# Attention: values in half pieces, k in rows of four keys, and another order for the first loads

## The chip, the cores and the metric

The kernel runs on one core of a Trainium2 chip. The metric is the device time of one execution in microseconds; of three runs the median counts. A core has five engines that work side by side, each with its own instruction queue: PE (matrix products), DVE (vector), ACT (activation functions), POOL and SP. SP does no arithmetic here; it issues DMAs. ACT issues some too. The DMAs of both queues run on the same 16 DMA engines. Engines wait for one another through semaphores.

## What is computed

Softmax attention for 16 x 32 = 512 heads in bfloat16, with 192 queries and 1024 keys of 128 elements in each head:

```python
B, H, Sq, Sk, D = 16, 32, 192, 1024, 128
scale = q.shape[-1] ** -0.5
scores = jnp.einsum("bhqd,bhkd->bhqk", q, k) * scale
p = _softmax(scores, axis=-1)
return jnp.einsum("bhqk,bhkd->bhqd", p, v)
```

The order of the keys doesn't matter, as long as a head's scores and its values are taken in the same order. k and v are 134 MB each, q and the output 25 MB each.

## The kernel before

**Tiles.** The heads are worked in 32 groups of 16 (`G`), a group in 8 pairs of heads, a pair in three units of 128 query rows: A (128 rows of one head), B (128 rows of the other) and S (64 rows of each). So there are 24 units a group. For a unit, PE multiplies q and k into 128x1024 scores in PSUM (`qk`, L270), DVE scales and copies them and finds each row's maximum in one instruction (L333), ACT takes the exponential (L374; for two units in six POOL subtracts the maximum first, L208, and ACT takes the exponential later), PE transposes the result in eight blocks of 128 keys (`tr`, L283), ACT brings the blocks back to SBUF (L383, L385), PE multiplies them by the values (`pv`, L317), and DVE divides by the row sums (L358). The order of the units on PE, DVE and ACT is written out by hand (`PE_ORDER` and its sisters, L17 to L20).

**Loads.** `kt` holds k transposed, `qt` q transposed, `vs` the values; each has two slots (`NS`), used by turns. k and q come by transposing DMAs on SP's queue (`load_kq`, L145), which put 128 elements of the head dimension on the partitions. A row of the k transpose is eight neighbouring keys (2048 bytes), so block t of a head's transposed keys has keys t, 8 + t, 16 + t and so on. The values come so that partition p has keys 8p to 8p + 7, one piece of 2048 bytes for each head and partition (`load_v`, L136). Both give the same order of keys.

**Order on SP.** After the start SP runs, for each group g: wait until the scores of group g are all done, issue k and q of group g + 2 into the slot that became free (`loads`, L157), then wait for group g's outputs and issue its stores in three DMAs by partitions (`stores`, L166, `STORE_PARTS`). The values of group g + 2 are issued by ACT, in its order of work, after unit 15 of group g + 1; it waits there until group g's products with values are done and until k of group g + 2 has landed (L391 to L394). A waiting instruction holds up everything behind it in its queue.

**The first two groups** have their own code. Group 0 comes in three parts by `FIRST`, heads 0 to 1, 2 to 7 and 8 to 15, in this order on SP's queue: k and q of the first part; k and q of the second; values of the first and of the second; k and q of the third; values of the third (L177 to L182). Group 1's k, q and values follow on the same queue. PE waits for each part's k and q before its first scores (L253) and for each part's values before its first product with them (L309).

Of the kernel before, what the change touches and what calls it, by code (L numbers as in the profile page):

```python
# [5 lines left out]
BF16 = mybir.dt.bfloat16  # L6
# [25 lines left out]


def _attention_kernel(nc, q, k, v, out, G=16, NS=2, NSS=5, NX=4, NPT=5,
                      FIRST=((0, 2), (2, 8), (8, 16)), LAST=((0, 4), (4, 6), (6, 7), (7, 8)), STORE_PARTS=((0, 80), (80, 124), (124, 128)), VALUES_AFTER=("ev", 15)):
    B, H, SQ, D = q.shape
    SK = k.shape[2]
    assert D == 128 and SK == 1024 and SQ == 192, (D, SK, SQ)
# [6 lines left out]
    KT_TILES = SK // 128  # L45
# [6 lines left out]
    kf = k.rearrange("b h s d -> (b h) s d")  # L52
    vf = v.rearrange("b h s d -> (b h) s d")
    of = out.rearrange("b h s d -> (b h) s d")

    def shifted(u):
        return UNITS[u % 6] in SHIFTED
# [12 lines left out]
    with ExitStack() as es:  # L70
        def sb(name, shape, dt):
            return es.enter_context(nc.sbuf_tensor(name, shape, dt))
# [4 lines left out]
        def sem(name):  # L77
            return es.enter_context(nc.semaphore(name))

        kt = sb("kt", [128, NS, KT_TILES, G * 128], BF16)  # L80
        qt = sb("qt", [128, NS, G * SQ], BF16)
        vs = sb("vs", [128, NS, G, KT_TILES, 128], BF16)
        ob = sb("ob", [128, NSO, PPG, 3, 128], BF16)
        ss = sb("ss", [128, NSS, SK], F32)
        nb = sb("nb", [128, NSS], F32)
# [11 lines left out]
        sxq = [sem("sxq%d" % i) for i in range(NS)]  # L97
        svl = [sem("svl%d" % i) for i in range(NS)]
        sf = [sem("sf%d" % i) for i in range(len(FIRST))]
        sfv = [sem("sfv%d" % i) for i in range(len(FIRST))]  # L100
        sst = [sem("sst%d" % i) for i in range(NSO)]
        s_qk = sem("s_qk")
        s_max = sem("s_max")
# [10 lines left out]
        def unit_info(u):  # L114
            name = UNITS[u % 6]
            pr = 2 * (u // 6) + int(name[1])
            return pr, "ABS".index(name[0]), pr // PPG, pr % PPG
# [6 lines left out]
        def load_cnt(g):  # L124
            return 16 * (g // NS + 1 - (g % NS == 0))
# [10 lines left out]
        def load_v(e, g, a, b, sm):  # L136
            h0 = g * G
            e.dma_start(  # L138
                vs[:, g % NS, a:b],
                vf[h0 + a:h0 + b].rearrange("g (p t) d -> p g t d", t=KT_TILES),  # L140
            ).then_inc(sm, 16)

        @block.sync
        def _(e):
            def load_kq(g, a, b, sems):  # L145
                s = g % NS
                h0 = g * G
                e.dma_start_transpose(  # L148
                    kt[:, s, :, a * 128:b * 128],
                    kf[h0 + a:h0 + b].rearrange("g (p t) d -> (g p) (t d)", t=KT_TILES),  # L150
                ).then_inc(sems[0], 16)
                e.dma_start_transpose(  # L152
                    qt[:, s, a * SQ:b * SQ],
                    qf[h0 + a:h0 + b].rearrange("g r d -> (g r) d"),
                ).then_inc(sems[1], 16)

            def loads(g):  # L157
                s = g % NS
                last_u = (g - NS + 1) * UPG - 1
                if g >= NS:  # L160
                    e.wait_ge(s_qk, last_u + 1)
                load_kq(g, 0, G, (sxk[s], sxq[s]))
                if g < NS:
                    load_v(e, g, 0, G, svl[s])

            def stores(g, a, b):  # L166
                so = g % NSO
                e.wait_ge(s_on, g * PPG + b)
                rows = of[g * G + 2 * a:g * G + 2 * b].rearrange("h r d -> (h r) d").rearrange(
                    "(n p) d -> p n d", p=128)  # L170
                for lo, hi in (((0, 128),) if g == NGR - 1 else STORE_PARTS):
                    e.dma_start(
                        rows[lo:hi],
                        ob[lo:hi, so, a:b].rearrange("p pg y d -> p (pg y) d"),
                    ).then_inc(sst[so], 16)

            n = len(FIRST)  # L177
            for i in range(n):
                load_kq(0, *FIRST[i], (sf[i], sf[i]))
                if i > 0:  # L180
                    for i2 in range(i if i > 1 else 0, i + 1):
                        load_v(e, 0, *FIRST[i2], sfv[i2])  # L182
            for g in range(1, min(NS, NGR)):
                loads(g)
            for g in range(NGR):
                if g + NS < NGR:
                    loads(g + NS)
                for a, b in (LAST if g == NGR - 1 else ((0, PPG),)):
                    stores(g, a, b)
            for so in range(min(NSO, NGR)):  # L190
                n = len(range(so, NGR - 1, NSO)) * len(STORE_PARTS)
                if so == (NGR - 1) % NSO:
                    n += len(LAST)
                e.wait_ge(sst[so], 16 * n)
# [23 lines left out]
        def _(pe):  # L218
# [19 lines left out]
            def qk(u):  # L238
                pr, k3, g, pg = unit_info(u)
                s = g % NS  # L240
                a = 2 * pg
                b = 2 * pg + 1
                S = s_ps[u % 2]
                if k3 < 2:
                    x0 = a * SQ if k3 == 0 else b * SQ + 64
                    tiles = [((0, 0), slice(0, 128), a if k3 == 0 else b, qt[:, s, x0:x0 + 128])]
                else:
                    tiles = [
                        ((0, 0), slice(0, 64), a, qt[:, s, a * SQ + 128:a * SQ + 192]),
                        ((0, 64), slice(64, 128), b, qt[:, s, b * SQ:b * SQ + 64]),  # L250
                    ]
                if g == 0:
                    for i, (h, _) in enumerate(FIRST):  # L253
                        if h <= b and i not in seen_kq:
                            seen_kq.add(i)
                            pe.wait_ge(sf[i], 32)
                elif u % UPG == 0:
                    pe.wait_ge(sxq[s], load_cnt(g))
                ins = None
                for c in range(2):  # L260
                    cs = slice(4 * c, 4 * c + 4)
                    for at, ps_, x, w in tiles:
                        if c == 0:
                            pe.ldweights(w, tile_position=at)  # L264
                            if at[1] == 0:
                                if g > 0 and u % UPG == 0:
                                    pe.wait_ge(sxk[s], load_cnt(g))
                                if u >= 2:
                                    pe.wait_ge(s_max, u - 1)
                        ins = product(S[ps_, cs], w, kt[:, s, cs, x * 128:x * 128 + 128], at)  # L270
                ins.then_inc(s_qk, 1)

            def tr(u):
# [12 lines left out]
            def pv(u):  # L286
                pr, k3, g, pg = unit_info(u)
                s = g % NS
                O = o_ps[pr % 2]
                PTS = pt_sb[:, u % NPT]  # L290
                sl = O_SLOT[k3]
                a = 2 * pg
                b = 2 * pg + 1
                ins = None
                with_rs = shifted(u)
                if k3 < 2:
                    tiles = [((0, 0), slice(0, 128), a if k3 == 0 else b)]
                else:
                    tiles = [((0, 0), slice(0, 64), a), ((0, 64), slice(64, 128), b)]
                pe.wait_ge(s_ev, u + 1)  # L300
                for t in range(KT_TILES):
                    first = t == 0
                    last = t == KT_TILES - 1
                    for at, rows, x in tiles:
                        w = PTS[:, t, rows]
                        pe.ldweights(w, tile_position=at)  # L306
                        if first and at[1] == 0:
                            if g == 0:
                                for i, (h, _) in enumerate(FIRST):  # L309
                                    if h <= b and i not in seen_v:  # L310
                                        seen_v.add(i)
                                        pe.wait_ge(sfv[i], 16)
                            elif u % UPG == 0:
                                pe.wait_ge(svl[s], load_cnt(g))
                            if k3 == 0 and pr >= 2:
                                pe.wait_ge(s_on, pr - 1)
                        ins = product(O[rows, sl, :], w, vs[:, s, x, t, :], at, first, last)  # L317
                        if with_rs:
                            ins = product(O[rows, 3, sl: sl + 1], w, ones[:, 0:1], at, False, last)
                ins.then_inc(s_pv, 1)  # L320
# [112 lines left out]
```

## Time and profile before

| | |
|---|---|
| three runs | 1200.33, 1194.54, 1207.98 us; median 1200.33 |
| the profiled execution | 1195.41 us, span 1193.6 |
| granted TensorE clock | 0.984 |
| busy: PE, DVE, ACT, POOL | 1127.5, 1088.2, 1082.4, 485.8 us |
| DMA | 321.26 MB, mean 269 GB/s |
| DMA from issue to landing, median | k 21.1, q 8.4, values on ACT's queue 16.3 us |

The span runs from the first to the last instruction of the profiled execution. "Busy" is the union of an engine's instructions. A line of a group or of the timeline has the source line (L148 is line 148), the engine (SPq is SP's queue), the operation and what it writes and reads (out<-in). In brackets stands the engine's idle time before it and what ended it. A row of the waits has the total, the number and the longest. DMA share is the mean busy share of the 16 DMA engines; it can pass 1, since pieces overlap. From the trace's record of single DMA pieces one can count how many of each size start in a stretch of time.

### The profile page before, as it was taken

The page shows a single profiled execution, that of the slowest core. Times are in us where ns is not written, and L with a number is a line of the kernel's source. Part 1 is how long each engine was busy: PE and PEld are TensorE (multiplying, and loading weights), DVE is VectorE, ACT ScalarE, POOL GpSimd, SP SyncE. Part 2 cuts the span into 40 slices and gives each one's busy share as a digit, 9 for nine tenths or more (in the row PEclk, how much of TensorE's full clock was granted, in tenths as well). Part 3 has the DMA queues.
Part 4 walks back from the last instruction along what each step waited for, and adds up shares of the span by engine and source line. Part 5 has one row for each costly group of instructions (what it writes and reads, how often), then busy time and mean ns, then how long its engine had stood idle before and what let it go on. Part 6 is the DMA issues. An engine that isn't in the chain of part 4 may idle for free.

```text
span 1193.6 us, 38884 instructions
## 1 busy us (share of the span) xinstructions
PE 1127.5 (94%) x18432; PEld 847.8 (71%) x15360; DVE 1088.2 (91%) x2304; ACT 1082.4 (91%) x1793; POOL 485.8 (41%) x262
## 2 busy tenths in 40 slices
PE   5698999999989999999999999999999999999998
PEld 2476767777767777777776777777777777777766
DVE  5587989999989999999998999999999999999987
ACT  4677989999999999999997999999999999999988
POOL 2233434434434434444443444444344344444432
PEclk9888999999999999999998999999999999999999
DMA  9999999999999999999999999999999999999991
GB/s 234 243 282 268 270 248 247 288 297 290 288 256 267 275 304 281 285 276 274 289 283 280 266 251 279 295 303 278 275 265 268 292 284 290 271 271 277 291 245 41
DMA packets 790348, 321.26 MB, mean 269 GB/s; under 512 B 724641, under 2 KB 724641, under 8 KB 790177
## 3 DMA queue, kind: packets, MB, share of 16 engines
q1 hardware_dynamic: 728257, 192.95, 83.9%
q10 hardware_dynamic: 61920, 125.83, 28.9%
q8 instruction: 132, 2.16, 0.7%
q14 instruction: 39, 0.32, 0.1%
HBM read 134.22 MB, written 25.17 MB: 134 GB/s over the span
## 4 chain that ended last, share of the span: by engine, by line
PE 58%; DMA 29%; ACT 7%; SPq 5%; issue 0%; DVE 0%
PE o_ps L221 21%; PE pt_ps L221 19%; DMA vs<-in_v_dram 19%; PE s_ps L221 18%; DMA qt<-in_q_dram 11%; SPq L148 5%; ACT x_sb L374 4%; ACT pt_sb L385 2%; ACT pt_sb L383 1%; SPq L152 0%; SPq L138 0%; DVE ob L358 0%; DVE rinv L356 0%
## 5 line engine op out<-in xcount | busy, mean ns | idle before, releaser
L333 DVE TENSOR_SCALAR_CACHE_REDUCE ss<-s_ps 128x1024 f32<-128x1024 f32 x768 | 920.4, 1220 | 89.1 <-PE s_ps L221 72.8
L208 POOL TENSOR_TENSOR x_sb<-ss,nb 128x1024 bf16<-128x1024 f32 x256 | 485.1, 1895 | 695.9 <-DVE ss L333 665.7
L374 ACT ACTIVATE x_sb<-ss,nb 128x1024 bf16<-128x1024 f32 x512 | 585.4, 1145 | 12.9 <-DVE ss L333 12.9
L306 PEld LDWEIGHTS <-pt_sb 128*128 128x128 bf16 (+1 forms) x8192 | 443.2, 104 | 213.5 <-issue 115.6
L221 PE MATMUL s_ps<-kt,qt 128*128 128x512 bf16 (+1 forms) x2048 | 467.9, 386 | 47.5 <-DMA qt<-in_q_dram 47.0
L221 PE MATMUL o_ps<-vs,pt_sb 128*128 128x128 bf16 (+1 forms) x8192 | 497.5, 219 | 14.2 <-DMA vs<-in_v_dram 13.9
L221 PE MATMUL pt_ps<-ident,x_sb 128*128 128x128 bf16 x6144 | 453.1, 220 | 1.3 <-ACT pt_sb L383 1.3
L280 PEld LDWEIGHTS <-x_sb 128*128 128x128 bf16 x6144 | 367.5, 98 | 62.5 <-issue 62.1
L385 ACT ACTIVATE pt_sb<-pt_ps 128x512 f32<-128x512 f32 x512 | 306.2, 598 | 78.7 <-PE pt_ps L221 77.8
L383 ACT ACTIVATE pt_sb<-pt_ps 128x1024 bf16<-128x1024 bf16 x256 | 260.4, 1017 | 14.4 <-PE pt_ps L221 14.3
L221 PE MATMUL o_ps<-ones,pt_sb 128*128 128x1 bf16 x2048 | 191.2, 166 | 0.0
L358 DVE TENSOR_TENSOR ob<-o_ps,rinv 128x384 bf16<-128x384 f32 x256 | 142.7, 557 | 8.8
L264 PEld LDWEIGHTS <-qt 128*128 128x128 bf16 (+1 forms) x1024 | 79.6, 104 | 66.6 <-DMA qt<-in_q_dram 44.0
L374 ACT ACTIVATION_READ_ACCUMULATOR x_sb<-ss,nb 128x1 f32 x512 | 100.7, 197 | 0.0
L333 DVE DVE_READ_ACCUMULATOR ss<-s_ps 128x1 f32 x768 | 63.8, 83 | 0.0
L356 DVE RECIPROCAL rinv<-o_ps 128x1 f32<-128x1 f32 x256 | 41.8, 163 | 4.2 <-PE o_ps L221 4.2
L346 DVE RECIPROCAL rinv<-rs 128x2 f32<-128x2 f32 x256 | 40.9, 160 | 1.1 <-ACT x_sb L374 1.1
L374 ACT ACT_TABLE_LOAD x1 | 1.3, 1283 | 0.8 <-PEq L418 0.8
L200 POOL TENSOR_SCALAR_AFFINE_SELECT ident<-ones 128x128 bf16<-128x128 bf16 x1 | 0.3, 295 | 0.1
L198 POOL MEMSET ones<- 128x128 bf16 x1 | 0.2, 205 | 0.3 <-POOLq L418 0.3
L418 POOL MEMSET const-float32-0.0<- 128x1 f32 x1 | 0.1, 100 | 0.3 <-issue 0.3
L418 POOL MEMSET const-uint8-127<- 128x1 uint8 x1 | 0.1, 103 | 0.0
(2 smaller groups left out, 0.2 us busy)
## 6 DMA issues: line engine op xcount, KB each, us to landing
vs<-in_v_dram ACTq DMA_DIRECT2D x30, 4096.0 KB, 16.3
out_dram<-ob SPq DMA_DIRECT2D x31, 480.0 KB
out_dram<-ob SPq DMA_DIRECT2D x31, 264.0 KB
vs<-in_v_dram SPq DMA_DIRECT2D x1, 4096.0 KB, 15.1
vs<-in_v_dram SPq DMA_DIRECT2D x1, 2048.0 KB, 9.9
vs<-in_v_dram SPq DMA_DIRECT2D x1, 1536.0 KB, 8.6
out_dram<-ob SPq DMA_DIRECT2D x31, 24.0 KB
kt<-in_k_dram SPq DMA_TRANSPOSE x34, 21.1
```

Source lines behind the costliest of these rows:

```text
L148: e.dma_start_transpose(kt[:, s, :, a * 128:b * 128], kf[h0 + a:h0 + b].rearrange("g (p t) d -> (g p) (t d)", t=KT_TILES),).then_inc(sems[ ...
L208: gp.tensor_tensor(x_sb[:, u % NX, :], ss[:, u % NSS, :], nb[:, u % NSS: u % NSS + 1].to_broadcast([128, SK]), ALU.subtract,).then_inc(s_x ...
L221: return pe.add_instruction(mybir.InstMatmult(name=nc.get_next_instruction_name(), engine=mybir.EngineType.PE, ins=[pe.lower_ap(x), pe.low ...
L264: pe.ldweights(w, tile_position=at)
L280: pe.ldweights(w, is_transpose=True, tile_position=(0, 0))
L306: pe.ldweights(w, tile_position=at)
L333: dve.tensor_scalar(ss[:, u % NSS, :], s_ps[u % 2][:].rearrange("p t k -> p (t k)"), -scale, None, ALU.mult, ALU.min, accum_out=nb[:, u % ...
L356: dve.reciprocal(rinv[:, pr % 2, sel], o_ps[pr % 2][:, 3, sel]).then_inc(s_ri, 1)
L358: dve.tensor_tensor(ob[:, so, pg], o_ps[pr % 2][:, 0:3, :], rinv[:, pr % 2, 0:3].unsqueeze(2).to_broadcast([128, 3, 128]), ALU.mult,).then ...
L374: act.activation(x_sb[:, u % NX, :], ss[:, u % NSS, :], ACT_FN.Exp, bias=nb[:, u % NSS: u % NSS + 1], scale=-1.0, accum_out=rs[:, pr % NRS ...
L383: act.activation(pt_sb[:, u % NPT], pt_ps[u % 2][:], ACT_FN.Exp, scale=-1.0).then_inc(s_ev, 1)
L385: act.activation(words(pt_sb[:, u % NPT]), words(pt_ps[u % 2][:]), ACT_FN.Copy).then_inc(s_ev, 1)
```

## The change

The values come in two halves of 512 keys. `vs` has 32 entries of 1024 bytes a group instead of 16 of 2048; partition p has keys 4p to 4p + 3 of the first half and 512 + 4p to 512 + 4p + 3 of the second, so that a DMA has twice as many pieces, of 1024 bytes. To match, a row of the k transpose is four keys (1024 bytes), with 256 rows a head instead of 128, and `kt` is 4 x 256 columns a head instead of 8 x 128. The scores' matmul reads two runs of 256 columns; the products with values take block t from half t % 2 and entry t // 2. The bytes are the same.

For group 0, `FIRST` has two parts, heads 0 to 1 and 2 to 15, and a new `FIRST_V` has two parts for the values, heads 0 to 7 and 8 to 15. SP issues all k and q first, then the two parts of the values.

```diff
-                      FIRST=((0, 2), (2, 8), (8, 16)), LAST=...
+                      FIRST=((0, 2), (2, 16)), FIRST_V=((0, 8), (8, 16)), LAST=...
...
-        kt = sb("kt", [128, NS, KT_TILES, G * 128], BF16)
+        kt = sb("kt", [128, NS, 4, G * 256], BF16)
         qt = sb("qt", [128, NS, G * SQ], BF16)
-        vs = sb("vs", [128, NS, G, KT_TILES, 128], BF16)
+        vs = sb("vs", [128, NS, 2 * G, 4, 128], BF16)
...
-                vs[:, g % NS, a:b],
-                vf[h0 + a:h0 + b].rearrange("g (p t) d -> p g t d", t=KT_TILES),
+                vs[:, g % NS, 2 * a:2 * b],
+                vf[h0 + a:h0 + b].rearrange("g (y p t) d -> p (g y) t d", y=2, t=4),
...
-                    kt[:, s, :, a * 128:b * 128],
-                    kf[h0 + a:h0 + b].rearrange("g (p t) d -> (g p) (t d)", t=KT_TILES),
+                    kt[:, s, :, a * 256:b * 256],
+                    kf[h0 + a:h0 + b].rearrange("g (p t) d -> (g p) (t d)", t=4),
...
-            n = len(FIRST)
-            for i in range(n):
-                load_kq(0, *FIRST[i], (sf[i], sf[i]))
-                if i > 0:
-                    for i2 in range(i if i > 1 else 0, i + 1):
-                        load_v(e, 0, *FIRST[i2], sfv[i2])
+            for i, (a, b) in enumerate(FIRST):
+                load_kq(0, a, b, (sf[i], sf[i]))
+            for i, (a, b) in enumerate(FIRST_V):
+                load_v(e, 0, a, b, sfv[i])
...
-                        ins = product(S[ps_, cs], w, kt[:, s, cs, x * 128:x * 128 + 128], at)
+                        ins = product(S[ps_, cs], w, kt[:, s, 2 * c:2 * c + 2, x * 256:x * 256 + 256], at)
...
-                                for i, (h, _) in enumerate(FIRST):
+                                for i, (h, _) in enumerate(FIRST_V):
...
-                        ins = product(O[rows, sl, :], w, vs[:, s, x, t, :], at, first, last)
+                        ins = product(O[rows, sl, :], w, vs[:, s, 2 * x + t % 2, t // 2, :], at, first, last)
```

More of the change, by code (lines that the diff above doesn't have):

```diff
@@ L34, in _attention_kernel @@
 def _attention_kernel(nc, q, k, v, out, G=16, NS=2, NSS=5, NX=4, NPT=5,
-                      FIRST=((0, 2), (2, 8), (8, 16)), LAST=((0, 4), (4, 6), (6, 7), (7, 8)), STORE_PARTS=((0, 80), (80, 124), (124, 128)), VALUES_AFTER=("ev", 15)):
+                      FIRST=((0, 2), (2, 16)), FIRST_V=((0, 8), (8, 16)), LAST=((0, 4), (4, 6), (6, 7), (7, 8)), STORE_PARTS=((0, 80), (80, 124), (124, 128)), VALUES_AFTER=("ev", 15)):
     B, H, SQ, D = q.shape
@@ L99, in _attention_kernel @@
         sf = [sem("sf%d" % i) for i in range(len(FIRST))]
-        sfv = [sem("sfv%d" % i) for i in range(len(FIRST))]
+        sfv = [sem("sfv%d" % i) for i in range(len(FIRST_V))]
         sst = [sem("sst%d" % i) for i in range(NSO)]
```

## The prediction, on record before the result

> **What bounds the kernel now.** I read first the page's slices and queue rows, then the work by stretches of one group, then the DMA queue's own timeline, then the waits.
>
> ```profile
> DMA  9999999999999999999999999999999999999991
> DMA packets 790348, 321.26 MB, mean 269 GB/s; under 512 B 724641, under 2 KB 724641, under 8 KB 790177
> q1 hardware_dynamic: 728257, 192.95, 83.9%
> q10 hardware_dynamic: 61920, 125.83, 28.9%
> ```
>
> The DMA engines are never free. q1 is SP's queue (k, q, stores), q10 ACT's (values). Of 790,348 pieces 724,641 are small: the k and q transposes and the stores move 256 bytes at a time, whatever the length of their rows.
>
> One group in mid kernel, cut at the points where the traffic changes (the last columns are the DMA share and GB/s):
>
> ```profile
> 578.70:599.40 20.70, 20.70 (x346) 15.77 (x279) 20.14 (x45) 20.10 (x34) 9.24 (x5) 1.00 1.24 233
> 601.50:604.00 2.50, 2.50 (x53) 1.80 (x49) 2.43 (x8) 2.44 (x4) 1.90 (x1) 1.00 0.98 360
> 604.50:613.50 9.00, 7.67 (x128) 5.64 (x105) 7.41 (x17) 7.45 (x13) 3.15 (x2) 1.00 1.07 372
> 613.50:616.00 2.50, 2.50 (x45) 2.15 (x34) 2.47 (x7) 2.50 (x5) 0.65 (x1) 1.00 0.83 208
> ```
>
> k moves at 233 GB/s, values alone at 360, values beside stores at 372, and while the last stores drain only 208. The issues in the same stretch, from the timeline, and who waits:
>
> ```profile
> 578.73 16.48 SPq L148 DMA_TRANSPOSE kt<-in_k_dram  x1
> 595.25 4.71 SPq L152 DMA_TRANSPOSE qt<-in_q_dram  x1
> 599.43 0.38 ACTq L138 DMA_DIRECT2D vs<-in_v_dram  x1
> 600.00 7.28 SPq L172 DMA_DIRECT2D out_dram<-ob  x2
> 605.83 0.59 PE L221 MATMUL s_ps<-kt,qt 128*128 128x512 bf16 x2 [1.43 <-DMA qt<-in_q_dram]
> ...
> 613.97 19.05 SPq L148 DMA_TRANSPOSE kt<-in_k_dram  x1
> ```
>
> SP never rests: k, q, stores, next k, 35.2 us a round. Its k issue should start when the scores of two groups before are done, yet at 613.97 it starts because the stores' issue has ended. So the loads set the pace. The compute alone would need 34.7 us a group: that is the distance from group 13's to 14's first maximum (500.43 to 535.13), a group in which PE waited for nothing. From group 5 to group 31 the mean is (1147.16 - 213.83) / 26 = 35.90, so 1.2 us a group, 31 us in all, are the loads' doing. The wait rows between 200 and 1150 us say which load is last:
>
> ```profile
> PE s_ps L221 <- DMA qt<-in_q_dram: 22.5, 16, 2.9
> PE o_ps L221 <- DMA vs<-in_v_dram: 5.9, 8, 1.7
> ```
>
> Mostly q, not the values. The first groups cost more: group 1 starts at 61.20 because its q lands at 60.04 (PE idle 10.42 us), and groups 1 to 5 lie 38.2 us apart, with PE waits on values of 3.7, 2.7 and 1.55 us.
>
> **The price of a piece.** Counting the trace's single DMA pieces: 256 bytes alone start at 1133 a microsecond, over 16 engines 14.1 ns each; 2048 bytes alone (62 to 69 us) at 192, 83 ns; side by side at 170 and 170, strictly one to one, 94 ns a pair. A straight line between 14.1 and 83 puts 1024 bytes at 43.6 ns. The ends are 41.5 (half of 83) and 83 (no cheaper at all); I take 43.6, as both neighbours lie on the same engines. Two halves then cost 87.2 instead of 83: with 128 pieces an engine and group, **+0.54 us of DMA time a group**; at the ends 0 and +10.6.
>
> The Trainium skill (DMA: Bandwidth & Descriptors, "Why small descriptors are slow") counts beats of 32 bytes plus about 3 cycles a packet: 35 against 67, two halves 4.5% dearer, an estimate by that page; the line gives 5%. Its table "Specifications" calls everything from 512 bytes up line rate; by that the half pieces would be free, and those rounds below that the DMA sets 0.5 us shorter, about 5 us in all.
>
> **k in rows of four keys.** As many 256-byte pieces as before. q, with rows of 256 bytes, and k, with rows of 2048, both run at 1133 pieces a microsecond where nothing disturbs them, so 1024 between them gets no other rate: 0. A bound from the same view: k took 19.8 to 22.0 us from issue to landing in undisturbed groups, so 1 us either way would be within what it shows; 26 us over all groups, kept in the range's ends only in part because both neighbours agree. The scores' moving operand becomes two runs of 256 columns instead of four of 128. No row shows another run length for 512 columns; the nearest are this one, 379 ns, and one run of 128, 219 ns. A tenth of 379 ns on 48 matmuls would be 1.8 us a group of PE time; longer runs can hardly cost that, and I take 0. Values are still read in runs of 128.
>
> **What the half pieces move.** Three things.
>
> (a) Stores pass faster. One to one, a store piece waits for 80 ns of values now and 44 then. But the work is the same sum, and the last stores, on fewer engines, end 17 us after the values' issue in both cases (256 x 43.6 + 240 x 14.1 ns = 14.5 us on the fullest engine, plus 2 us until values flow). What may be gained is the gap in which stores drain and k has not begun: 2.5 us at 208 instead of about 290 GB/s, 0.7 us a group at most.
>
> (b) The values' pieces must be queued first. From 601.5 to 604.0 only values move. SP's queue is dry until some 440 to 500 of the 2048 pieces have left (counted in 18 groups; also where a code fetch delays them to 6 us after the issue), and it isn't dry where the stores were issued before the values (groups 3, 4, 22). At the end of every k issue about 1,700 pieces are outstanding, 106 an engine. I read it so: a queue holds about 100 pieces an engine, and no other DMA is laid out until the one before it is. With 128 pieces 28 must leave first, 28 x 83 = 2.3 us; with 256 it is 156 x 43.6 = 6.8 us. q's tail is what is caught: in such groups q lands 5.4 us after the values' issue, so then at 9.9. The first maximum comes 0.75 us later and the next values' issue 28.5 us after that: 39.2 us instead of 34.7 for that round. In the next round k is ahead of the values by 3.8 us, q escapes, and the round costs the compute's 34.7. But there k meets the values one to one (as at 91 to 129 us), k lands some 38 us after the one before, and the lead is 0.4; one more round by the DMA uses it up: values' issue to values' issue takes 35.4, 35.0 and 35.1 us where nothing else was late (564 to 599, 1034 to 1104), plus 0.54, less 0.4 of (a): 35.3. Mean of 39.2, 34.7 and 35.3: 36.4, **+0.5 us x 26 = +13 us**. Ends: without any such queueing (a) and the price of a piece alone, 35.2 us a group, -17; caught every second round, (39.2 + 34.7) / 2 = 36.95, +28.
>
> (c) Early groups. There stores go ahead of the values and k is beside them; values land 19.7, 18.8 and 17.6 us after issue. With small pieces and SP held back, 120 store pieces take 60 ns a pair (7.2 us), the next 36 go alone (1.6), the last 100 beside k at about 70 (7.0): with 1.9 to the first piece 17.7. That frees up to 2 us of PE's wait on values in two groups: **-4 us**, between -8 (all three waits gone) and +4 (k beside values as slow as at 100 to 110 us, where only 126 pieces of values a microsecond passed).
>
> **The first group.** Now pairs 1 to 3 start at 13.85, when their k and q are in, and pairs 4 to 7 at 30.84; PE is done at 49.7 and waits until 60.15. With heads 2 to 15 in one load, k runs at full rate from 7.25 us: 14,336 + 2,688 pieces less the 1,400 already gone, at 1133 a microsecond, 13.8 us, plus 1.2 for the change from k to q seen at 12 us: q lands at 22.4. Everything after the first pair starts 8.6 us later, and this would be the loss if nothing covered it. The cover is PE's idle 10.42 us before group 1: the work needs 32.6 us without its waits and ends at 55. The first values (heads 0 to 7) are issued behind q at about 20.5 and land at about 29.5, the first product with them is due 8.1 us after the start, 30.6: no wait, though only by a microsecond. Group 1's k and q come behind the same bytes with fewer changes between loads: v for heads 8 to 15 at 36.3 instead of 37.58, q of group 1 at 58.8. **-1.3 us**, between -3 and +3. No instruction or wait of the compute engines is added; ACT issues one DMA as before, taken in 0.38 us though it exceeds the queue, as the stores' 0.58 us shows.
>
> **Sum.** -1.3 - 4 + 13 = +7.7 on the profiled 1195.41 us (span 1193.6 and 1.8 around it), 1203. The runs' median, 1200.33, lies 4.9 higher, so **1208**.
>
> **Rivals.**
> - *The queue serves both* (faster): descriptors of q and stores are laid out beside the values', the burst is as short as now or shorter, q is out by 4.2 us, and DMA paces at 35.2 or the compute at 34.7 to 34.9. -1.3 - 8 - 17 to -26: about 1170. For it: the alternation one to one; against it: SP's dry 2.5 us in nearly every group.
> - *q caught every second or every round* (slower): it decides as soon as q's issue ends later than 0.35 us before the values' issue; now k's landing, which releases the values, precedes the end of q's issue by 0.5, so every round without a lead is caught. Every second: +28 - 5, 1223; every round (39.2): +86, about 1280. Against the latter: a late round gives k a lead.
> - *k in shorter rows isn't as fast, or 1024 bytes cost far more than the line*: 1 us a group, +30, 1230.
> - *The first group loses its cover*: values too late, +5 at most.
>
> **Chances.** A measurement of this kernel tells about 1% (12 us) from no change; the three runs spread over 1.1%. Forecast, within 1% (1188 to 1212): 0.38. Slower (queue, k rows): 0.36. Faster (queue serves both): 0.26. The range takes in the faster case down to 1172 and the slower up to 1236; beyond are the compute floor and q caught in every round, about one in ten each. The forecast's own range is 1190 to 1214.
>
> **What will show it.** First score after the first pair near 22.4 us; PE's 10 us idle before group 1 shrunk to 4, group 1 at about 60. In each group a stretch of values alone of nearly 7 us at about 375 GB/s (2.5 if the queue serves both). Waits on q fewer but longer, up to 6 us. Values' landing after issue 16 to 18 us. k from issue to landing still 20 to 22 us undisturbed; if it moves by over 1 us, the step on rows is wrong. I am wrong altogether if q lands less than 5 us after the values' issue in most groups, or if waits on values overtake those on q.

## The result, and the profile after

The changed kernel takes 1294.63 us (median of four runs, 1282.32 to 1301.17). The kernel before took 1197.43 beside it (four runs, 1189.12 to 1207.98). The ratio is 1.0825, 95% interval 1.070 to 1.095: 8% slower, well outside the predicted range of 1172 to 1236. Where some executions of a kernel ran slower at a lower granted clock, the medians below take in all of them, and the ratios and the table at the end of the experiments only the others. The profiled execution took 1301.17 us, span 1299.4, with a mean granted clock of 0.957 (before 0.984).

The page's slices, queues and chain of the kernel after:

```profile
DMA  9999999999999999999999999999999999999991
DMA packets 855804, 321.26 MB, mean 247 GB/s; under 512 B 724561, under 2 KB 855633, under 8 KB 855633
q10 hardware_dynamic: 123360, 125.83, 31.8%
DMA 47%; PE 34%; ACT 15%; SPq 4%; issue 0%; DVE 0%
```

The change is there: ACT's queue q10 has twice the pieces with the same bytes. The DMA engines are still never free, but they move 247 GB/s instead of 269. On the chain that ended last, DMA now holds 47%; before it held 29% and PE 58%.

The wait rows between 200 and 1150 us, the stretch that the prediction read (total, number, longest):

```profile
DVE ss L332 <- PE s_ps L220: 119.0, 42, 7.4
PE o_ps L220 <- DMA vs<-in_v_dram: 93.5, 24, 6.3
```

Before, q stood first with 22.5 us and the values had 5.9. Now the values have 93.5, and there is no row for q in this stretch. DVE's row is an echo: PE, stopped at a product with values, delivers no scores.

The sum over the whole span closes. PE waits 117.1 us for values instead of 13.9 (+103.2) and 24.1 us for q instead of 47.0 (-22.9): 80.3 us more rest. PE's busy time grew from 1127.5 to 1153.2 us with the same 18,432 matmuls: 25.7 us. Together 106.0, and the span grew by 105.8.

The DMA issues of the kernel after (number, KB each, median us from issue to landing):

```profile
vs<-in_v_dram ACTq DMA_DIRECT2D x30, 4096.0 KB, 20.6
...
kt<-in_k_dram SPq DMA_TRANSPOSE x33, 30.6
qt<-in_q_dram SPq DMA_TRANSPOSE x33, 6.1
```

Values land 20.6 us after their issue (before 16.3), k 30.6 (before 21.1). Both are slower, and they now move at the same time. One round in the timeline, from the end of group 10's k (landed at 407.93) to group 11's k:

```profile
404.35 4.22 SPq L153 DMA_TRANSPOSE qt<-in_q_dram  x1
408.62 3.93 SPq L173 DMA_DIRECT2D out_dram<-ob  x3
414.52 0.37 ACTq L139 DMA_DIRECT2D vs<-in_v_dram  x1
418.99 25.02 SPq L149 DMA_TRANSPOSE kt<-in_k_dram  x1
...
431.91 0.22 PE L220 MATMUL o_ps<-vs,pt_sb 128*128 128x128 bf16 x1 [1.30 <-DMA vs<-in_v_dram]
```

Before, in most groups, the order was k, q, values, stores, next k, without a gap on SP: the values were issued 0.08 us after k had landed, and the next k came 14.5 us after the values. Here q and the stores go out first, SP rests from 412.55, ACT issues the values 6.6 us after k landed, and the next k follows them after 4.46 us, as soon as the group's scores are done. Over groups 5 to 31 the medians are 4.4 us from k's landing to the values' issue and 4.46 us from there to the next k; the distance from one group's first maximum to the next is 39.85 us instead of 35.90. 3.95 us times 26 is 103 us, nearly all of the 105.8.

The same round by stretches (length, busy time of PE, of its weight loads, of DVE, ACT and POOL; the last three columns are the granted clock, the DMA share and GB/s):

```profile
414.50:415.50 1.00, 1.00 (x17) 0.88 (x16) 0.97 (x5) 1.00 (x3) 0.69 (x1) 1.00 0.08 18
416.00:423.00 7.00, 7.00 (x126) 5.42 (x102) 6.86 (x15) 6.76 (x13) 2.96 (x2) 1.00 1.04 350
423.50:430.00 6.50, 6.50 (x116) 5.05 (x100) 6.43 (x13) 6.26 (x12) 2.23 (x2) 1.00 1.16 274
432.00:447.00 15.00, 15.00 (x258) 11.52 (x219) 13.47 (x29) 13.28 (x22) 6.15 (x4) 1.00 1.29 241
```

A microsecond in which almost nothing moves, values alone at 350 GB/s, then values beside k at 274, and the rest of k at 241. This is one of the milder rounds: PE waits 1.30 us. In the rounds on either side it waits 5.33 and 4.70 us.

**One thing more is in the trace: the clock after a wait.** Around PE's wait of 7.17 us for the values of group 29:

```profile
1183.50:1189.20 5.70, 0.00 (x0) 0.00 (x0) 0.62 (x2) 0.85 (x2) 0.57 (x1) 0.56 1.22 169
1189.30:1191.30 2.00, 1.92 (x25) 1.85 (x16) 0.00 (x0) 0.00 (x0) 0.00 (x0) 0.50 1.28 291
1191.30:1194.00 2.70, 2.70 (x21) 1.90 (x17) 1.23 (x2) 1.02 (x1) 0.00 (x0) 0.50 1.27 290
1194.00:1198.00 4.00, 4.00 (x70) 2.78 (x64) 3.07 (x7) 2.94 (x5) 1.90 (x1) 0.94 1.28 290
```

PE starts again at half clock and has it back only about 5 us later. This follows every wait on values of 4.3 us or more in this trace (17 of them, 0.50 to 0.64 over the next 4 us), two of the three between 3.0 and 3.4, and none of the eleven shorter ones. It makes up the 25.7 us of longer matmuls: PE was busy for 81.5 us at half clock instead of 26.7, and half of the difference is 27 us. The Trainium skill (TensorE: Matmul & The Clock Gate, "HAM oscillation — how this bites in real kernels") says that PE must not rest longer than some 3.4 us, or it is throttled to half; for the long waits the trace agrees, while rests of 3.10 and 3.06 us here, and of 2.71 us in the kernel before (0.63 over the next 4 us), were followed by it too.

### The profile page after: what moved, and what is told of

Same layout as the page of the kernel before. It is cut to its first block, busy times and chain, and to the rows that moved or that the text cites. A ratio compares the mean times of both kernels' runs of the same rounds, so it can differ in the third digit from the quotient of the medians.

```text
span 1299.4 us, 38881 instructions
## 1 busy us (share of the span) xinstructions
PE 1153.2 (89%) x18432; PEld 867.6 (67%) x15360; DVE 1089.3 (84%) x2304; ACT 1083.4 (83%) x1793; POOL 485.8 (37%) x262
## 3 DMA queue, kind: packets, MB, share of 16 engines
q8 instruction: 132, 2.16, 0.7%
## 4 chain that ended last, share of the span: by engine, by line
DMA 47%; PE 34%; ACT 15%; SPq 4%; issue 0%; DVE 0%
DMA vs<-in_v_dram 47%; PE o_ps L220 13%; PE pt_ps L220 11%; PE s_ps L220 10%; ACT x_sb L373 8%; ACT pt_sb L384 4%; SPq L149 3%; ACT pt_sb L382 2%; SPq L153 1%; SPq L139 0%; DVE ob L357 0%; DVE rinv L355 0%
## 5 line engine op out<-in xcount | busy, mean ns | idle before, releaser
L305 PEld LDWEIGHTS <-pt_sb 128*128 128x128 bf16 (+1 forms) x8192 | 454.5, 105 | 324.4 <-issue 228.6
L220 PE MATMUL o_ps<-vs,pt_sb 128*128 128x128 bf16 (+1 forms) x8192 | 509.2, 221 | 117.2 <-DMA vs<-in_v_dram 117.1
L220 PE MATMUL s_ps<-kt,qt 128*128 128x512 bf16 (+1 forms) x2048 | 475.6, 391 | 24.6 <-DMA qt<-in_q_dram 24.1
L220 PE MATMUL pt_ps<-ident,x_sb 128*128 128x128 bf16 x6144 | 460.8, 223 | 1.3 <-ACT pt_sb L382 1.3
L279 PEld LDWEIGHTS <-x_sb 128*128 128x128 bf16 x6144 | 375.9, 99 | 62.5 <-issue 62.1
L220 PE MATMUL o_ps<-ones,pt_sb 128*128 128x1 bf16 x2048 | 195.6, 168 | 0.0
## 6 DMA issues: line engine op xcount, KB each, us to landing
vs<-in_v_dram ACTq DMA_DIRECT2D x30, 4096.0 KB, 20.6
vs<-in_v_dram SPq DMA_DIRECT2D x1, 4096.0 KB, 16.3
kt<-in_k_dram SPq DMA_TRANSPOSE x33, 30.6
```

The source lines that it names most:

```text
L220: return pe.add_instruction(mybir.InstMatmult(name=nc.get_next_instruction_name(), engine=mybir.EngineType.PE, ins=[pe.lower_ap(x), pe.low ...
L279: pe.ldweights(w, is_transpose=True, tile_position=(0, 0))
```

## The experiments

Three questions: which part of the change costs the time; whether it is the price of the pieces or the order in which transfers meet; and whether the order can be put right. All comparisons are with the kernel before in runs beside them.

**Parts of the change.** First the halves without the new first order, and the new first order without the halves.

```diff
-  FIRST=((0, 2), (2, 16)), FIRST_V=((0, 8), (8, 16))          # after
+  FIRST=((0, 2), (2, 8), (8, 16)), FIRST_V=((0, 2), (2, 8), (8, 16))
   # and the start of before: k and q of a part, then its values
```

> Half pieces and rows of four keys, but the first group in the old order (heads 0-1, 2-7, 8-15 with their values between). Theory A (late values: half pieces are passed one to one by twice as many k pieces, so the values land some 20 us after issue instead of 16, PE waits for them in every group, and k of the next group is again issued beside them): 1280 to 1300 us, PE waits on values 100 us or more. Theory B (the new first order sets off the late state, the pieces matter little): 1195 to 1215, waits on values under 30 us. Theory C (pieces simply cost more engine time, 46 ns each instead of 84 for two, +1 us a group, and nothing else): 1225 to 1240.

Measured: 1291.31 us (1287.55 to 1297.88), ratio 1.084 (1.075 to 1.092). PE's waits on values 111.0 us, values 20.1 and k 30.6 us from issue to landing, 39.76 us a group. The same as the whole change.

```diff
-  FIRST=((0, 2), (2, 8), (8, 16))                             # before, 2048 bytes
+  FIRST=((0, 2), (2, 16)), FIRST_V=((0, 8), (8, 16))
   # and the start of after: all k and q, then the values
```

> Only the new first order, with 2048-byte pieces and k in rows of eight. A and C: 1193 to 1200 (group 1 about 2 us earlier, nothing else). B: 1280 to 1300.

Measured: 1196.93 us (1179.83 to 1220.7), ratio 0.996 (0.989 to 1.003). No difference that this tells. In its trace group 1 starts at 57.92 instead of 61.20, so some 3 us are won at the head. The loss lies in the halves.

Next, which half of the halves: k in rows of four with values in pieces of 2048 bytes, and value halves with k in rows of eight. In both, a head's scores and values are taken in different orders of keys; the work and the bytes are the same.

```diff
-  vs = sb("vs", [128, NS, 2 * G, 4, 128], BF16)               # after
+  vs = sb("vs", [128, NS, G, KT_TILES, 128], BF16)            # k stays in rows of four
```

> Only k in rows of four keys; the values come in 2048-byte pieces of eight keys as before, so scores and values belong to different keys and the output isn't the reference's; the work is the same. A: as the new order alone, 1185 to 1210. Rival E (the k transpose in short rows is what costs): 1270 or more, k landing later where nothing is beside it.

Measured: 1188.4 us (one run; 1194.91 beside it). Its DMA issues:

```profile
vs<-in_v_dram ACTq DMA_DIRECT2D x30, 4096.0 KB, 16.2
...
kt<-in_k_dram SPq DMA_TRANSPOSE x33, 20.9
```

Both land as before. The rows of k cost nothing.

```diff
-  kt = sb("kt", [128, NS, 4, G * 256], BF16)                  # after
+  kt = sb("kt", [128, NS, KT_TILES, G * 128], BF16)           # values stay in halves
```

> Only the values in half pieces of 1024 bytes; k in rows of eight keys as before, so scores and values belong to different keys and the output isn't the reference's; the work is the same. A: the whole loss, 1275 to 1305, PE waits on values about 100 us. E: 1190 to 1215.

Measured: 1294.28 us (one run), the whole loss. Its waits:

```profile
PE o_ps L220 <- DMA vs<-in_v_dram: 104.1, 30, 7.0
PE s_ps L220 <- DMA qt<-in_q_dram: 23.9, 3, 14.2
```

So it is the 1024-byte pieces of the values and nothing else in the change.

**Is it k beside the values?** SP's next k issue is held until the values have landed.

```diff
 # after, in loads(), before k's issue
+  e.wait_ge(svl[(g - 1) % NS], load_cnt(g - 1))
```

> The changed kernel, and SP waits before each k issue from group 2 on until the values of the group before have landed, so that k and values never share the engines; it adds a wait to SP with k, q and the stores queued behind it. A: values land in 13 to 15 us, PE waits on values under 40 us, k late instead by about 1 us a group: 1210 to 1235. C: no gain, and the wait costs its own 1 to 2 us a group, 1300 to 1340. B: as C.

Measured: 1245.57 us (1241.6 to 1248.99), ratio 1.046 (1.039 to 1.053). Its waits:

```profile
PE s_ps L221 <- DMA qt<-in_q_dram: 54.4, 25, 14.1
...
PE o_ps L221 <- DMA vs<-in_v_dram: 44.2, 26, 3.2
```

Half the loss comes back. With no k beside them the values land after 17.6 us instead of 20.6, but now k starts 17.7 us after the values' issue, and q is late instead. Even alone with the stores, the values take more than the 16.3 us of before and PE still waits for them 26 times.

**Is it that the values come late?** ACT issues the values after unit 12 instead of 15, in both layouts.

```diff
-  VALUES_AFTER=("ev", 15)                                     # after
+  VALUES_AFTER=("ev", 12)
```

> The changed kernel with the values' issue on ACT after unit 12 of the group instead of 15, 4.3 us earlier in ACT's order. A: the loop values' landing, products, next issue is 4.3 us shorter, the values go ahead of the stores, PE waits on values fall from 117 us to under 50: 1210 to 1245. C: 1285 to 1300, since the engines' time is the bound. B: as C.

Measured: 1210.47 us (1204.17 to 1214.43), ratio 1.016 (1.008 to 1.024). 84 of the 97 us are gone, with the same half pieces. Its waits:

```profile
ACT pt_sb L384 <- DMA kt<-in_k_dram: 35.0, 14, 3.6
PE s_ps L220 <- DMA qt<-in_q_dram: 23.8, 3, 14.1
...
PE o_ps L220 <- DMA vs<-in_v_dram: 6.4, 6, 1.9
```

ACT now waits at the values' issue until k has landed, in every group from 2 on (0.08 us from landing to issue). So the end of q and the stores come behind the values and no longer ahead; the next k is issued 10.7 us after the values (median) instead of 4.46. The values land after 18.0 us, and PE hardly waits for them: 36.77 us a group.

```diff
-  VALUES_AFTER=("ev", 15)                                     # first order of after, 2048 bytes
+  VALUES_AFTER=("ev", 12)
```

> 2048-byte pieces and rows of eight as before, the new first order, and the values' issue after unit 12 instead of 15. A: the values are then always issued as k lands, also in groups 2 to 5, whose excess of 14 us over 34.7 a group falls by half or more: 1183 to 1193, and not slower than the order alone (1197). If an earlier issue is no cure but only another way for k and values to share: 1200 to 1215.

Measured: 1185.6 us (ten runs, 1179.64 to 1191.47), ratio 0.9956 (0.9921 to 0.9991). This is 0.4% below the kernel before, with an interval just below 1. The new first order alone had the same ratio, 0.996, so no gain from the earlier issue itself is shown. Its waits:

```profile
PE s_ps L219 <- DMA qt<-in_q_dram: 23.4, 3, 14.0
ACT pt_sb L383 <- DMA kt<-in_k_dram: 23.3, 11, 3.0
```

There is no row of PE waiting on the values any more. The values land after 16.2 us, the next k is issued 14.7 us after them, 35.85 us a group. Against the half pieces with the same order (36.77) this leaves 0.92 us a group, 24 us over 26 groups: that is what the small pieces cost with this order. The other 84 us between 1210 and 1295 belong to the issue after unit 15. An earlier issue changes two things, the order and the time at which the values start; the run with k held, further down, separates them.

**The same order with large pieces.** If lateness is what costs the 84 us, pieces of 2048 bytes must pay it too when the issue is moved later.

```diff
-  VALUES_AFTER=("ev", 15)                                     # first order of after, 2048 bytes
+  VALUES_AFTER=("ev", 19)
```

> 2048-byte pieces and rows of eight, the new first order, the values' issue after unit 19 instead of 15, 5.8 us later in ACT's order. A (the state is one of lateness, not of piece size): it falls into the same state as the changed kernel, values landing late in every group, k issued 4 to 5 us after the values and landing 30 us after its issue, 1270 to 1340. Rival D (only small pieces can make k and values hinder each other so): a wait of a few us in the first groups, then as before, 1200 to 1225.

Measured: 1612.61 us (one run). The direction is right and the size far off (1270 to 1340 was expected). k is issued 1.07 us ahead of the values and goes beside them over their whole length; they land after 24.9 us, and PE waits 401.5 us, 13 us a group, with the clock at a mean of 0.862.

```diff
-  VALUES_AFTER=("ev", 15)                                     # first order of after, 2048 bytes
+  VALUES_AFTER=("ev", 17)
```

> 2048-byte pieces, rows of eight, the new first order, the values' issue after unit 17, about 2 us later than after unit 15: as much as the half pieces delayed the landing (18.0 instead of 16.2 us where the order was the same). A2: it tips into the late state, 1270 to 1400, k issued about 4 us or less after the values. If more lateness than that is needed (5.8 us gave 1613): 1195 to 1225.

Measured: 1312.68 us (one run), within what was expected. Its waits on values and its issues:

```profile
PE o_ps L219 <- DMA vs<-in_v_dram: 100.3, 30, 4.1
```

```profile
vs<-in_v_dram ACTq DMA_DIRECT2D x30, 4096.0 KB, 16.8
```

The waits are as large as those of the changed kernel, with the pieces of before, and k again goes beside the values: they are issued 8.2 us after k's landing, the next k 1.8 us after them, k takes 30.5 us, 40.28 us a group. But the values themselves land after 16.8 us, hardly later than the 16.2 of the good order. What PE waits for here is the issue, which stands 2.65 us later against the group's first maximum (3.45 us ahead of it instead of 6.10). So this run shows that a later issue has no room, and not that the order alone makes large pieces slow.

**And a little earlier with half pieces.**

```diff
-  VALUES_AFTER=("ev", 15)                                     # after
+  VALUES_AFTER=("ev", 14)
```

> The changed kernel with the values' issue after unit 14, about 1.7 us earlier, what the half pieces cost in landing. A2: most of the loss goes, 1205 to 1245, waits on values under 50 us. If the late state needs the 4 us of unit 12 to break: 1260 to 1300.

Measured: 1209.31 us (1203.17 to 1217.88), ratio 1.015 (1.006 to 1.024). One unit, about 1.45 us, is worth 85 us, by the earlier issue and the order together. This trace shows both orders in one run. In groups 2 to 8 the values are issued within 0.22 us of k's landing and the next k 10 to 13 us later. In group 9 q and the stores get ahead: values 1.7 us behind k, next k 6.0 us after them, values landing after 22.2 us, PE waiting 4.62 us. It stays so for groups 10 and 11 (3.16 and 6.41 us) and is back at 0.08 us in group 13. So the late order sustains itself for some rounds, but not without end.

**Holding k a fixed while, without the earlier issue.**

```diff
 # after, in loads(), before k's issue: unit 1 of the next group has to be through ACT
+  e.wait_ge(s_ev, last_u + 3)
```

> The changed kernel; SP waits before each k issue also until ACT has brought back unit 1 of the next group (about 14.5 us after the values' issue, where k was issued before the change), which holds q and the stores behind it. A2: k no longer runs beside the values, they land in 17 to 17.6 us as with the full wait, but k starts at once behind them: 1205 to 1230. If k's place beside the values isn't what keeps them late: 1270 or more.

Measured: 1226.96 us (1219.57 to 1234.12), ratio 1.030 (1.022 to 1.037). The next k is issued 15.5 us after the values. Its DMA issues:

```profile
vs<-in_v_dram ACTq DMA_DIRECT2D x30, 4096.0 KB, 17.8
...
kt<-in_k_dram SPq DMA_TRANSPOSE x33, 20.4
```

Some 68 of the 97 us are back with the values' issue where it was. Together with the hold until landing (1245.57), this shows that k beside the values (with q and the stores, which stand behind k in SP's queue) is the main carrier of the loss, and that keeping it away has its own price on the other side.

**Quarters.** Values in four entries of 512 bytes, k in rows of two.

```diff
-  vs = sb("vs", [128, NS, 2 * G, 4, 128], BF16)               # after
+  vs = sb("vs", [128, NS, 4 * G, 2, 128], BF16)
-  vf[...].rearrange("g (y p t) d -> p (g y) t d", y=2, t=4)
+  vf[...].rearrange("g (y p t) d -> p (g y) t d", y=4, t=2)
```

> Values in quarters of 256 keys (512-byte pieces, four times as many as before) and k in rows of two keys, the rest as the changed kernel. A2 (the queues are served one piece each by turns, so a smaller piece is a smaller share for the values, and late values keep themselves late): values land 24 to 28 us after issue, some 45 us a group, 1430 to 1550. Rival F (a step: below 2048 bytes it is the same state whatever the size): 1285 to 1320.

Measured: 1363.11 us (one run), between the two ranges given. But it isn't the experiment it was meant to be. Its queue row:

```profile
q10 hardware_dynamic: 61920, 125.83, 34.8%
```

The trace has as many value pieces as with 2048 bytes, of 2048 bytes each, and not four times as many. Half of them take 113 ns or more instead of 84; alone some 140 start in a microsecond instead of 185 to 188. So the share per piece was that of before and only the price was higher. It still has the late order (values 4.9 us behind k's landing, next k 4.4 us after them, landing after 20.8 us, PE waiting 150.2 us on them). So a higher price of the pieces was enough to bring this order (k's rows of two keys were changed with it, and no run takes the two apart); it says nothing on smaller shares.

The times by the unit after which ACT issues the values, all with the first order of after:

| | unit 12 | 14 | 15 | 17 | 19 |
|---|---|---|---|---|---|
| 2048 bytes | 1185.6 | | 1188.6 | 1312.7 | 1612.6 |
| 1024 bytes | 1210.5 | 1209.3 | 1294.6 | | |

Both layouts have an edge. The one before stood on its safe side by less than two units; the half pieces move it by enough to fall over. Past the edge the time is not lost in the same way: with 2048 bytes after unit 17 it is the later issue, with half pieces after unit 15 it is the slower landing (20.6 us).

## Why the prediction was wrong

**What happens.** A queue's share goes by pieces. In stretches where value pieces and store pieces both flow, 167 of each start in a microsecond with 2048 bytes and 279 of each with 1024. The values' part of the engines' time falls, the stores' rises. Stores and q are through some 4 us earlier, so the next k comes 10.7 instead of 14.7 us after the values (issue after unit 12 in both), and its pieces too go ahead of value pieces: counted over such rounds, about 3,600 foreign pieces pass before the last value piece, not 2,600. The values land after 18.0 us instead of 16.2. Of these 1.8 us the price of the pieces gives about 1.0 (128 pairs an engine, 92 ns instead of 84) and the thousand further foreign pieces about 0.9 (14.1 ns each over 16 engines); these are estimates from the counts, and no run separates the two. In the kernel before they were due about then: the first product comes 9.9 us after the group's first maximum, and the values landed 9.4 to 10.5 us after it in groups 6 to 16. There was hardly anything to spare. The same shows in the loop from one values' issue to the next: from the values' landing, ACT needs 18.67 us to reach the next issue where only the values held it up and the clock was full. With 16.4 us of landing (mean of groups 5 to 30) that makes 35.1 of the 35.90 us of a group; with 18 us it is more than a group. So PE waits, after long waits runs at half clock, and ACT reaches the next values' issue later. By then k has landed and q and the stores have gone ahead, so the next k follows the values within 4.46 us and goes beside them. They land after 20 us, and PE waits again. The kernel before was in this order in groups 2 to 4 (PE waits 3.68, 2.71, 1.55 us) and left it in group 5 (and was in it for group 18 alone, 0.92 us); the kernel after has 5.62, 5.52, 0.40 there, and then 3.10, 5.16, 2.16, 5.98.

In the kernel after the loop sets the pace: a mean of 19.98 us of landing and 19.87 us to the next issue (18.67, and up to 2.8 more after long waits) are its 39.85 us a group. That the order makes the larger part of the loss is shown by the run with k held: the values' issue stays after unit 15, they land after 17.8 us, and 68 of the 97 us come back. The earlier issues bring back 84 and 85, but shorten the loop by themselves too. That the half clock helps to keep it up is argued from the trace and was not tried by itself.

By the prediction's steps:

- **The price of a piece: right in kind, about half in size (+0.54 us a group).** Half pieces take 46 ns each, 92 for two against 84; the straight line said 87.2 against 83. That is 1.0 us a group by these durations, and the runs with the values issued in order measured 0.92. The Trainium skill's estimate of 4.5% that the prediction gave (DMA: Bandwidth & Descriptors, "Why small descriptors are slow") is low by half; its table "Specifications", by which they would be free, is not what this trace shows.
- **k in rows of four at 0: right.** With that part alone k took 20.9 us from issue to landing, and the kernel 1188.4 us.
- **(a), stores pass faster: this step failed.** It saw that a store piece waits 44 ns instead of 80 and asked only when the last store would end: "17 us after the values' issue in both cases". It did not ask what the values lose by it, left the next k where it was, and took nothing for the wait that follows. Values later by 1.8 us and the next k earlier by 4 us were in the same rates of one to one, and the price, that it quoted. In the place of its mean of 36.4 us a group the loop through the values took 39.85.
- **(b), the values' pieces queued first: wrong reading.** It took SP's dry stretch for 28 pieces an engine that must leave, so 156 with half pieces. Where the stores are issued right behind the values, SP's pieces come again about 4.9 us after the values' issue with 1024 bytes (some 1,000 pieces gone) and 4.65 us with 2048 (some 480): the same time and the same megabyte, no count of pieces. q is not caught longer; its wait row of 200 to 1150 us is gone. The stretch of values alone of "nearly 7 us" came true in the round above and for another reason: there SP has nothing to send, and a k issued 4.46 us after the values moves its first piece 4.3 us later (in the 14 of 29 rounds in which SP's queue was empty by then; in the others pieces of SP's queue went on within 0.6 us, and stores and k can't be told apart by size).
- **(c), early groups: wrong sign.** For -4 us it had the values landing after 17.7; they take 21.7 and 21.6 us in groups 2 and 3. The step had the right scene, k beside the values, and treated it as something that ends by itself.
- **The first group, -1.3: right.** The second k and q land at 22.83 (22.4 predicted), the first values at 29.59 (29.5), the rest at 35.53 (36.3), q of group 1 at 58.09 (58.8), and group 1 starts at 59.25: -1.95. (The terms for q, 7.25, 13.8 and 1.2, add up to 22.25.)
- **The rivals.** None had this one. "q caught in every round" came near in size (1280), by another mechanism. The last clause, wrong altogether "if waits on values overtake those on q", names the row that came. The clause ahead of it came as well: q landed less than 5 us after the values' issue in all 30 groups. But that was so in 13 of 30 before, so it told little.
- **What the reading of the profile missed.** The row `PE o_ps L221 <- DMA vs<-in_v_dram: 5.9, 8, 1.7` was taken as "not the values". Short waits in eight groups of 26 say that the values land just when they are due, and groups 2 to 4 showed what comes of it when they don't.

## What to carry to other kernels

A row of many short waits isn't slack: it marks a transfer that lands just in time, and a cost of 1 us there is to be followed through the next rounds, to what is issued earlier or later because of it. Where two queues share the DMA engines piece by piece, the size of a piece sets the queue's share, so halving the pieces of the urgent transfer slows it beside the other queue (here the values moved 0.342 MB/us beside the stores with 2048 bytes and 0.286 with 1024). Before a change near such an edge, move the issue a unit earlier and later: here one unit earlier took back 85 of the 97 us. And when such a move loses, look whether the transfer itself became slower or only started later.

## What the runs showed of the hardware

- The two queues alternate by single pieces whatever their size: 167 and 167 a microsecond with 2048 beside 256 bytes, 279 and 279 with 1024 beside 256. With 2048 bytes issued after unit 12, 16 of any 32 successive starts are the values' (standard deviation 0.4, counted 9 to 12 us after their issue). The sum moved falls from 0.385 to 0.357 MB/us.
- Values beside k's transposes moved 0.27 MB/us (median of the rounds of the kernel after, from k's first piece to the last value piece), less than beside stores of the same 256 bytes. In half of the half-microseconds it was 0.34 or more, so the loss lies in stops of a microsecond or two of both and in tails in which few value pieces are left. Why is open.
- Where SP's queue had run dry, the first pieces of a DMA issued on it behind the 4 MB of values came about 4.2 to 4.4 us after its own issue (medians of five runs), whatever had gone by then: stores with about 1 MB of the values gone, with either size of piece; k with 1.6 MB gone (2048 bytes, unit 17) and with 2.0 to 2.7 MB (the kernel after, 14 rounds).
- PE waits of 4.3 us and more were followed by half clock for 3 to 6 us, 25.7 us of longer matmuls in all, a quarter on top of the 103.2 us by which the waits themselves grew.
- Entries of 512 bytes were recorded as pieces of 2048 bytes that took 113 ns (median) instead of 84.
